# Attention weights written out by head through three buffers, a narrower second form of the value tails, and the lists judged at the last step's end

## The chip, the cores and the metric

The kernel runs on one core of one Trainium2 chip. The metric is the device time of one execution in microseconds (us). Before the change it took 1482.36 us (median of three runs, 1481.56 to 1483.75).

The core's engines work side by side, each in the order of its own queue: TensorE (PE; its weight loads are listed as PEld), VectorE (DVE), ScalarE (ACT), GpSimd (POOL), and SyncE (SP), which issues all of this kernel's DMAs. An engine that waits holds up everything queued behind it on that engine.

## The reference

Attention that keeps the 32 largest scores of every row, and then a two-layer MLP with the SmeLU function. Shapes: batch 8, heads 8, sequence 576, head size 64; the MLP goes from 512 to 2048 and back.

```python
scores = scale * np.matmul(q, k.transpose(0, 1, 3, 2))
kth = np.partition(scores, -top_k, axis=-1)[..., -top_k:-top_k + 1]
mask = scores >= kth
scores = np.where(mask, scores, -1000000000.0)
scores = scores - np.max(scores, axis=-1, keepdims=True)
attn = np.exp(scores)
attn = attn / (np.sum(attn, axis=-1, keepdims=True) + 1e-09)
attn_out = np.matmul(attn, v)
x = attn_out.transpose(0, 2, 1, 3).reshape(B * S, H * D)
h = x @ w_in
g = np.where(h >= 1, h, np.where(h <= -1, 0.0, (h + 1) ** 2 / 4.0))
out = g @ w_out
```

## The kernel before

**Steps.** A sequence of 576 rows is four tiles of 128 rows (t = 0 to 3) and a tail of 64 (t = NT = 4). A step treats one tile of rows for two heads, or in a tail for four heads, two of them in each half of the partitions. There are 144 steps. The batches go in pairs: four tiles of the first batch, the tails of both, then four tiles of the second. `i` counts the two rows of work that lie side by side in a step's tiles `s` (scores) and `e` (weights).

**One step, engine by engine.** PE multiplies queries by keys (L358) and ACT copies the scores to `s` (L359). DVE folds each row in two halves of 288 (`more` and `less`, L372) and looks for the 32 largest with MAX8 and MATCH_REPLACE8 (L379, L392 to L446). ACT takes the exponential (L395). A scan over the two sorted lists (L451) gives the 32nd value, and L458 keeps the weights at or above it and adds them up. POOL divides by the sum (L411) and notes in `excess` whether the lists were long enough (L414).

**How the weights are turned.** The product with the values needs the weights transposed. In the first steps and in the last two (`by_tensor`), PE does this with a diagonal of the reciprocal sums (`diag`, made by ACT at L408, then L473 and L479). In the other 134 steps `move_w` does it through memory: ACT copies the two rows' weights, split in their upper and lower 16 bits, to one tile `halves` (L488, one copy for each `i`); SP writes this tile to DRAM as `rows` (L490) and reads it back transposed as `wT` (L492), once `rows` has landed. Tiles of one tag share buffers: `halves` and `diag` are both of the tag "halves", with one buffer. `wT` has four, `rows` three.

**Products and MLP.** `values` multiplies `wT` by the values (`po`, L506 for the four tiles and L514 for the tails), ACT copies the outcome to `xT` (L519, L521). Once all heads of a tile of rows are there, `mlp` adds its work to a list: `hidden` (`ph`, L539, with its functions on ACT L550 and L558 and on POOL L565 to L568) and `final` (`py`, L578). The output `y` (L581) leaves by SP (L583).

**Tails of the values.** The last 64 rows of the values lie in two forms for each batch. In `v_tl[0]` the even heads lie in partitions 0 to 63 and the odd ones in 64 to 127 (L198, two loads). In `v_tl[1]` the pairs of heads alternate between the two halves (L203, four loads, with a `yield` after each second one). The other half of the partitions is zero in both. The four tiles take the first form, the tails' steps the second. `v_tails` (L84) holds two sets, for even and odd batches.

**Order.** The order on PE, DVE, ACT and POOL is written out by hand: a loop over the steps m, with seven slots in each. `weights` runs a piece of DVE's work in each slot; slot 1 holds `transpose_w`, slot 3 `move_w` of the step before, slot 2 the scores and values. In each slot `advance` takes as much of the MLP's list as the step's share allows, by counted costs, so the MLP is spread over the steps. Keys and queries of the batches from the third on are turned through memory too: `turn` copies them by ACT (`parts`, L283), SP writes them (L285) and reads them back transposed (L292). The loads of keys (L303 to L307), values (L195 to L203) and queries (L211) lie in SP's queue between the steps' transposes, most of them around the change from one pair of batches to the next.

**Judging the lists.** `judge` subtracts counts for the MLP's weights (L864), takes the largest entry of `excess` on DVE (L865), turns it on PE (`pworst`, L867), and takes the largest again (L869). The `flag` that comes of it decides at the very end whether the whole is done once more in a slower way. `judge` is called in slot 2 at m = n, after the last step's diagonals were multiplied and before its values.

Of the kernel before, what the change touches and what calls it, by code (L numbers as in the profile page):

```python
# [11 lines left out]
F32 = mybir.dt.float32  # L12
U16 = mybir.dt.uint16
# [13 lines left out]
def kernel(  # L27
# [10 lines left out]
    nc = tc.nc  # L38
    B, H, S, D = q.shape
    NTOK, DM = out.shape  # L40
    DFF = moe_w_in.shape[1]
    P = 128
# [3 lines left out]
    NHP = H // 2  # L46
    NT = S // P
    SM = NT * P
    TL = S - SM
# [10 lines left out]
    const = ctx.enter_context(tc.tile_pool(name="const", bufs=1))  # L60
# [20 lines left out]

    v_tails = []
    for i in range(2):
        v_tails.append([const.tile([P, H, D], F32, name=f"v_tail{i}{x}") for x in range(2)])  # L84
        for x in v_tails[i]:
            nc.gpsimd.memset(x, 0.0)

# [89 lines left out]
    def run(ctx, paired):  # L177
# [4 lines left out]
        dram = ctx.enter_context(tc.tile_pool(name="dram", bufs=3, space=bass.MemoryType.DRAM))  # L182
# [3 lines left out]
        def whole(x, b):  # L186

            return x[b, :, 0:SM, :].rearrange("h (p c) d -> p h c d", c=NT)

        def load_values(b):  # L190
            v_in = stage.tile([P, H, NT, D], F32, name="v_in")
            v_tl = v_tails[b % 2]
            yield v_in, v_tl
            for h in range(0, H, 2):
                nc.sync.dma_start(out=v_in[:, h:h + 2], in_=whole(v, b)[:, h:h + 2])  # L195
                yield
            for j in range(2):
                nc.sync.dma_start(out=v_tl[0][j * TL:(j + 1) * TL, j::2, :],  # L198
                                  in_=v[b, j::2, SM:S, :].rearrange("h p d -> p h d"))
            yield  # L200
            for hp in range(NHP):
                g = hp % 2
                nc.sync.dma_start(out=v_tl[1][g * TL:(g + 1) * TL, 2 * hp:2 * hp + 2, :],  # L203
                                  in_=v[b, 2 * hp:2 * hp + 2, SM:S, :].rearrange("h p d -> p h d"))
                if g:
                    yield

        def load_queries(b, t):
            if t < NT:
# [14 lines left out]
        def part(i, j):  # L224
            return slice(0, TL) if i == j else slice(TL, P)
# [64 lines left out]
        def finish_turns():  # L290
            while turns:
                turns.pop(0)()  # L292
# [109 lines left out]
        def divide(st):  # L402
            rz = att.tile([P, 2], F32, name="rz")
            nc.vector.reciprocal(rz, st["z"])  # L404
            if st["by_tensor"]:
                st["rz"] = diag = (late or words).tile([P, 2, P], F32, name="diag", tag="halves", bufs=1)
                for i in range(2):
                    nc.scalar.activation(diag[:, i, :], ident, AF.Copy, scale=rz[:, i:i + 1])  # L408
            else:
                for i in range(2):  # L410
                    nc.gpsimd.tensor_scalar(st["e"][:, i, :], st["e"][:, i, :], rz[:, i:i + 1], 1.0, ALU.mult, ALU.mult)  # L411
            if paired:
                m, seconds, kth = st["m"], st["seconds"], st["kth"]
                nc.gpsimd.tensor_tensor(out=excess[:, 2 * m:2 * m + 2], in0=seconds[:, 8:9 + SPLIT:SPLIT], in1=kth[:, LAST:7:-SPLIT],  # L414
                                        op=ALU.subtract)

        def weights(st, before, after):
# [44 lines left out]
            if after is None:  # L462
                divide(st)
# [19 lines left out]

        def move_w(st):
            st["wT"] = wT = late.tile([P, BLOCKS, P], F32, name="wT", bufs=4)
            halves = late.tile([P, 2, 2 * S], U16, name="halves")
            for i in range(2):
                nc.scalar.copy(halves[:, :, i * S:(i + 1) * S], st["e"][:, i, :].bitcast(U16).rearrange("p (k t) -> p t k", t=2))  # L488
            rows = dram.tile([P, 2, 2 * S], U16, name="rows")
            nc.sync.dma_start(out=rows, in_=halves)  # L490
            finish_turns()
            nc.sync.dma_start_transpose(wT.bitcast(U16), rows.rearrange("p t k -> (p t) k"))  # L492

        def block(i, c):
            return i * (NT + 1) + c if c < NT else NT


        def values(st):
            t, hp, v_in, v_tl = st["t"], st["hp"], st["keys"]["v"], st["keys"]["v_tl"]
            wT = st["wT"]  # L500
            po = ps.tile([P, P], F32, name="po", tag="ph", bufs=3)
            if t < NT:
                for c in range(NT + 1):
                    for j in range(2):
                        h = 2 * hp + j
                        nc.tensor.matmul(po[j * D:(j + 1) * D], v_in[:, h, c, :] if c < NT else v_tl[0][:, h, :],  # L506
                                         wT[:, block(j, c)], start=(c == 0), stop=(c == NT))
            else:
                for i in range(2):
                    cols = slice(i * TL, (i + 1) * TL)  # L510
                    for c in range(NT + 1):
                        for j in range(2):
                            h = 2 * (hp + i) + j
                            nc.tensor.matmul(po[j * D:(j + 1) * D, cols], v_in[:, h, c, :] if c < NT else v_tl[1][:, h, :],  # L514
                                             wT[:, block(i, c), part(i, j)],
                                             start=(c == 0), stop=(c == NT))
            xT, col = st["xT"]
            if t < NT:
                nc.scalar.copy(xT[:, hp, col:col + P], po)  # L519
            else:  # L520
                nc.scalar.copy(xT[:, hp:hp + 2, col:col + TL], po.rearrange("p (i n) -> p i n", i=2))  # L521
# [80 lines left out]
        for b in range(0, B, 2):  # L602
            a, c, tl = [(b, t) for t in range(NT)], [(b + 1, t) for t in range(NT)], (b, NT)
# [9 lines left out]
        n = len(steps)  # L613
# [5 lines left out]
        words, late = conversion.enter_context(tc.tile_pool(name="words", bufs=1)), None  # L619
# [32 lines left out]
        K_TIME, PIECE_TIME, UNIT_TIME, SLOTS, EARLY_SHARE = 10.1, 0.9, 0.218, 7, 48  # L652
# [113 lines left out]
        for m in range(n + 2):  # L766
# [3 lines left out]
            elif not early and late is None:  # L770
                conversion.close()
                room.clear()
                late = ctx.enter_context(tc.tile_pool(name="late", bufs=1))
# [15 lines left out]
            for slot in range(SLOTS):  # L789
# [17 lines left out]
                    ready_at[m - 1] = done[m - 1] + 15.0  # L807
                if slot == 3:
                    finish_turns()
                if slot == 2 and m == n and paired:  # L810
                    judge(ps, att)
                if slot == 2 and (early or m == first_late or m >= n - 1):
                    values_until(m)
# [48 lines left out]
    def judge(ps, att):  # L862
        worst = att.tile([P, 8], F32, name="worst", bufs=1)
        nc.vector.tensor_tensor(out=excess[:, 2 * n_steps:], in0=signs[:, 0], in1=signs[:, 1], op=ALU.subtract)  # L864
        nc.vector.max(out=worst, in_=excess)  # L865
        pt = ps.tile([1, P], F32, name="pworst", tag="a", bufs=2)
        nc.tensor.transpose(pt, worst[:, 0:1], ident)  # L867
        top = att.tile([1, 8], F32, name="top8", bufs=1)
        nc.vector.max(out=top, in_=pt)  # L869
        nc.vector.tensor_scalar(flag, top, 0.0, None, ALU.is_gt)  # L870
# [34 lines left out]
```

## Time and profile before

| what | value |
|---|---|
| median of three runs | 1482.36 us |
| the profiled execution | 1484.11 us |
| its span, first to last instruction | 1482.2 us |
| mean granted TensorE clock | 0.992 |
| HBM read, written | 62.91 MB, 102.63 MB |

A group's line has the source line, engine and operation, output<-input, shapes and count, then busy time in all and the mean of one in ns, then the idle time before it:

```profile
L488 ACT COPY halves<-e 128x1152 uint16<-128x1152 uint16 x268 | 293.6, 1143 | 18.5 <-DMA rows<-halves 18.1
L411 POOL TENSOR_SCALAR e<-e,rz 128x576 f32<-128x576 f32 x268 | 235.9, 890 | 13.2 <-DVE rz L404 13.2
```

The list of DMA issues gives the count, the size of one, and the median time from issue to landing in us:

```profile
rows<-halves SPq DMA_DIRECT2D x134, 576.0 KB, 3.3
...
wT<-rows SPq DMA_TRANSPOSE x134, 4.7
...
v_tail<-in_v_dram SPq DMA_DIRECT2D x16, 64.0 KB, 3.9
v_tail<-in_v_dram SPq DMA_DIRECT2D x32, 32.0 KB, 3.4
```

In a timeline a line starts with the start and the duration in us; the bracket at its end holds the idle time before and what ended it. "SPq" is SP's queue: the time is that of issuing, not of the transfer.

### The profile page before, as it was taken

The page shows a single profiled execution, that of the slowest core. Times are in us where ns is not written, and L with a number is a line of the kernel's source. Part 1 is how long each engine was busy: PE and PEld are TensorE (multiplying, and loading weights), DVE is VectorE, ACT ScalarE, POOL GpSimd, SP SyncE. Part 2 cuts the span into 40 slices and gives each one's busy share as a digit, 9 for nine tenths or more (in the row PEclk, how much of TensorE's full clock was granted, in tenths as well). Part 3 has the DMA queues.
Part 4 walks back from the last instruction along what each step waited for, and adds up shares of the span by engine and source line. Part 5 has one row for each costly group of instructions (what it writes and reads, how often), then busy time and mean ns, then how long its engine had stood idle before and what let it go on. Part 6 is the DMA issues. An engine that isn't in the chain of part 4 may idle for free.

```text
span 1482.2 us, 32086 instructions
## 1 busy us (share of the span) xinstructions
PE 1435.8 (97%) x10755; PEld 1044.6 (70%) x10755; DVE 1403.9 (95%) x4392; ACT 1158.0 (78%) x2221; POOL 926.6 (63%) x1310
## 2 busy tenths in 40 slices
PE   6998899999999999999999999999999999999998
PEld 5766677777777777767777777677777777777675
DVE  6989999999999999999999999999999999999912
ACT  7987877878888887887778888788778888777632
POOL 3474566776676666566766677567666666666730
PEclk8999999999999999999999999999999999999999
DMA  8633657775677767787677787787677886665510
GB/s 252 196 121 107 177 152 203 196 194 162 167 206 204 193 193 205 193 209 174 163 195 203 196 198 194 195 214 183 174 197 187 202 202 167 168 166 142 149 25 17
DMA packets 510319, 260.94 MB, mean 176 GB/s; under 512 B 460992, under 2 KB 469184, under 8 KB 510144
## 3 DMA queue, kind: packets, MB, share of 16 engines
q1 hardware_dynamic: 510144, 258.80, 66.4%
q8 instruction: 87, 1.43, 0.4%
q14 instruction: 88, 0.72, 0.2%
HBM read 62.91 MB, written 102.63 MB: 112 GB/s over the span
## 4 chain that ended last, share of the span: by engine, by line
PE 80%; DVE 10%; DMA 4%; ACT 4%; issue 2%; SPq 1%; ACTq 0%; DVEq 0%
PE ph L539 30%; PE py L578 29%; PE sp L358 9%; PE po L506 9%; DVE more L379 2%; DMA rows<-halves 2%; DVE e L458 2%; DMA wT<-rows 1%; PE po L514 1%; DVE more L372 1%; DVE tops L420 1%; DVE tops L428 1%; DVE tops L392 1%; PE pw L473 1%; ACT halves L488 1%
## 5 line engine op out<-in xcount | busy, mean ns | idle before, releaser
L539 PEld LDWEIGHTS ph<-xT,w_in 128*128 128x128 f32 x4608 | 547.0, 192 | 102.6 <-issue 71.1
L539 PE MATMUL ph<-xT,w_in 128*128 128x128 f32 x4608 | 555.7, 276 | 2.3 <-ACT g L558 1.4
L578 PE MATMUL py<-w_out,g 128*128 128x512 f32 x1152 | 541.5, 597 | 1.8 <-ACT y L581 1.8
L565 POOL TENSOR_SCALAR r<-r 128x256 f32<-128x256 f32 x280 | 166.9, 596 | 413.4 <-ACT r L550 409.7
L379 DVE MATCH_REPLACE8 more<-tops,more 128x288 f32<-128x288 f32 x864 | 375.1, 437 | 0.0
L578 PEld LDWEIGHTS py<-w_out,g 128*128 128x128 f32 x1152 | 199.0, 191 | 166.5 <-issue 163.8
L488 ACT COPY halves<-e 128x1152 uint16<-128x1152 uint16 x268 | 293.6, 1143 | 18.5 <-DMA rows<-halves 18.1
L568 POOL TENSOR_TENSOR g<-r,g 128x256 f32<-128x256 f32 x280 | 241.6, 863 | 22.0
L458 DVE SCALAR_TENSOR_TENSOR e<-s,kth,e 128x577 f32<-128x577 f32 x288 | 246.9, 893 | 0.1
L411 POOL TENSOR_SCALAR e<-e,rz 128x576 f32<-128x576 f32 x268 | 235.9, 890 | 13.2 <-DVE rz L404 13.2
L395 ACT ACTIVATE e<-s,nmax 128x576 f32<-128x576 f32 x288 | 222.5, 773 | 4.7
L550 ACT ACTIVATE r<-ph,half 128x256 f32<-128x256 f32 (+1 forms) x296 | 136.1, 460 | 107.8 <-PE ph L539 99.7
L359 ACT ACTIVATE s<-sp 128x576 f32<-128x576 f32 x288 | 171.9, 649 | 61.7 <-PE sp L358 57.7
L567 POOL TENSOR_TENSOR r<-r 128x256 f32<-128x256 f32 x276 | 183.1, 663 | 23.0
L358 PE MATMUL sp<-kT,qT 64*128 64x288 f32 x1024 | 163.1, 436 | 8.3 <-ACT kT L261 6.1
L506 PE MATMUL po<-wT,v_in 128*64 128x128 f32 x2048 | 138.8, 277 | 8.0 <-DMA wT<-rows 4.6
L358 PEld LDWEIGHTS sp<-kT,qT 64*128 64x128 f32 x1024 | 90.0, 189 | 79.3 <-issue 37.2
L506 PEld LDWEIGHTS po<-wT,v_in 128*64 128x64 f32 x2048 | 113.6, 137 | 32.4 <-issue 10.3
L558 ACT ACTIVATE g<-ph,minus 128x256 f32<-128x256 f32 x280 | 130.4, 466 | 0.0
L372 DVE TENSOR_TENSOR more<-s 128x576 f32<-128x576 f32 x144 | 124.1, 862 | 6.0 <-ACT s L359 6.0
L420 DVE MAX8 tops<-more 128x8 f32<-128x288 f32 x288 | 125.4, 443 | 0.0
L372 DVE TENSOR_TENSOR less<-s 128x576 f32<-128x576 f32 x144 | 117.7, 817 | 0.0
(91 smaller groups left out, 1370.0 us busy)
## 6 DMA issues: line engine op xcount, KB each, us to landing
rows<-halves SPq DMA_DIRECT2D x134, 576.0 KB, 3.3
lines<-parts SPq DMA_DIRECT2D x48, 256.0 KB, 3.1
q_in<-in_q_dram SPq DMA_DIRECT2D x32, 256.0 KB, 3.8
v_in<-in_v_dram SPq DMA_DIRECT2D x32, 256.0 KB, 4.5
out_dram<-y SPq DMA_DIRECT2D x32, 256.0 KB, 3.9
raw<-in_moe_w_in_dram SPq DMA_DIRECT2D x32, 256.0 KB, 3.3
raw<-in_moe_w_out_dram SPq DMA_DIRECT2D x32, 256.0 KB, 3.5
kT<-in_moe_w_in_dram SPq DMA_DIRECT2D x8, 512.0 KB, 5.2
```

What stands on the lines that cost most here:

```text
L358: nc.tensor.matmul(*x, start=True, stop=True)
L372: nc.vector.tensor_tensor(out=x, in0=s[:, :, 0:SH], in1=s[:, :, SH:S], op=op)
L379: nc.vector.match_replace(out=st["rest"][:, i, :], in_to_replace=eight(st["tops"], i, r - 8), in_values=src[:, i, :], imm_value=LOWEST)
L395: nc.scalar.activation(e[:, i, :], s[:, i, :], AF.Exp, bias=nmax[:, i:i + 1])
L411: nc.gpsimd.tensor_scalar(st["e"][:, i, :], st["e"][:, i, :], rz[:, i:i + 1], 1.0, ALU.mult, ALU.mult)
L458: nc.vector.scalar_tensor_tensor(out=st["all"][1][:, i, :], in0=st["all"][0][:, i, :], scalar=last[i], in1=st["all"][1][:, i, :], op0=ALU. ...
L488: nc.scalar.copy(halves[:, :, i * S:(i + 1) * S], st["e"][:, i, :].bitcast(U16).rearrange("p (k t) -> p t k", t=2))
L506: nc.tensor.matmul(po[j * D:(j + 1) * D], v_in[:, h, c, :] if c < NT else v_tl[0][:, h, :], wT[:, block(j, c)], start=(c == 0), stop=(c == ...
L539: nc.tensor.matmul(ph[:, i], w_in[:, kk, f * P:(f + 1) * P], xT[:, kk], start=(kk == 0), stop=(kk == NK - 1))
L567: nc.gpsimd.tensor_tensor(out=r, in0=r, in1=r, op=ALU.mult)
L568: nc.gpsimd.tensor_tensor(out=g, in0=r, in1=g, op=ALU.add)
L578: nc.tensor.matmul(py[0], gs[f // group][:, f % group], w_out[:, f, :], start=(f == 0), stop=(f == NF - 1))
```

## The change

The tile `halves` holds one row of work (`i`) instead of two, has three buffers, and each is written to its half of `rows` by a DMA of its own, right after its copy. `diag` shares these three buffers. The second form of the value tails keeps only the four heads (1, 2, 5, 6) that lie in the other half of the partitions than in the first form, and is loaded by two DMAs; a new function `tail_values` chooses the form by head. `judge` is called in the last slot of the last step (m = n + 1), after the last values.

```diff
-        v_tails.append([const.tile([P, H, D], F32, name=f"v_tail{i}{x}") for x in range(2)])
+        v_tails.append([const.tile([P, H // (x + 1), D], F32, name=f"v_tail{i}{x}") for x in range(2)])
...
             yield
-            for hp in range(NHP):
-                g = hp % 2
-                nc.sync.dma_start(out=v_tl[1][g * TL:(g + 1) * TL, 2 * hp:2 * hp + 2, :],
-                                  in_=v[b, 2 * hp:2 * hp + 2, SM:S, :].rearrange("h p d -> p h d"))
-                if g:
-                    yield
+            for x in range(2):
+                nc.sync.dma_start(out=v_tl[1][x * TL:(x + 1) * TL, x::2, :],
+                                  in_=v[b, x + 1::4, SM:S, :].rearrange("h p d -> p h d"))
+            yield
+
+        def tail_values(v_tl, h, t):
+
+            if t == NT and h % 2 != h // 2 % 2:
+                return v_tl[1][:, h // 4 * 2 + h // 2 % 2, :]
+            return v_tl[0][:, h, :]
...
-                st["rz"] = diag = (late or words).tile([P, 2, P], F32, name="diag", tag="halves", bufs=1)
+                st["rz"] = diag = (late or words).tile([P, 2, P], F32, name="diag", tag="halves",
+                                                          bufs=3 if late else 1)
...
         def move_w(st):
             st["wT"] = wT = late.tile([P, BLOCKS, P], F32, name="wT", bufs=4)
-            halves = late.tile([P, 2, 2 * S], U16, name="halves")
+            rows = dram.tile([P, 2, 2 * S], U16, name="rows")
             for i in range(2):
-                nc.scalar.copy(halves[:, :, i * S:(i + 1) * S], st["e"][:, i, :].bitcast(U16).rearrange("p (k t) -> p t k", t=2))
-            rows = dram.tile([P, 2, 2 * S], U16, name="rows")
-            nc.sync.dma_start(out=rows, in_=halves)
+                halves = late.tile([P, 2, S], U16, name="halves", bufs=3)
+                nc.scalar.copy(halves, st["e"][:, i, :].bitcast(U16).rearrange("p (k t) -> p t k", t=2))
+                nc.sync.dma_start(out=rows[:, :, i * S:(i + 1) * S], in_=halves)
             finish_turns()
...
-                        nc.tensor.matmul(po[j * D:(j + 1) * D], v_in[:, h, c, :] if c < NT else v_tl[0][:, h, :],
+                        nc.tensor.matmul(po[j * D:(j + 1) * D], v_in[:, h, c, :] if c < NT else tail_values(v_tl, h, t),
...
-                            nc.tensor.matmul(po[j * D:(j + 1) * D, cols], v_in[:, h, c, :] if c < NT else v_tl[1][:, h, :],
+                            nc.tensor.matmul(po[j * D:(j + 1) * D, cols], v_in[:, h, c, :] if c < NT else tail_values(v_tl, h, t),
...
-                if slot == 2 and m == n and paired:
+                if slot == SLOTS - 1 and m == n + 1 and paired:
                     judge(ps, att)
```

## The prediction, made before the changed kernel was run

> **What bounds the kernel now.** I read the page's totals first, then the chain that ended last, then the waits of each engine, then the timelines of SP, ACT and PE where those waits lie.
>
> ```profile
> PE 1435.8 (97%) x10755; PEld 1044.6 (70%) x10755; DVE 1403.9 (95%) x4392; ACT 1158.0 (78%) x2221; POOL 926.6 (63%) x1310
> ...
> PE 80%; DVE 10%; DMA 4%; ACT 4%; issue 2%; SPq 1%; ACTq 0%; DVEq 0%
> ```
> ```profile
> 1160.00:1180.00 20.00, 20.00 (x137) 13.80 (x136) 20.00 (x63) 15.73 (x30) 11.98 (x18) 1.00 0.89 200
> ```
> ```profile
> 1080.54 0.20 DVE L451 TENSOR_TENSOR_SCAN kth<-tops,seconds 128x25 f32<-128x25 f32 x1
> ...
> 1382.79 0.23 DVE L451 TENSOR_TENSOR_SCAN kth<-tops,seconds 128x25 f32<-128x25 f32 x1
> ```
>
> PE is 97% busy, and the chain runs on PE for 80% of the span. The third line is one of the stretches of 20 us (PE, PEld, DVE, ACT, POOL, clock, DMA share): PE and DVE are both full. The two scans, one per step, lie 32 steps apart: 302.25 / 32 = 9.445 us a step. I set the end of each step's score copy (L359) beside its first use (L372): DVE finds the scores 4 us old or older from 200 us on, so it never waits for PE. Over these 32 steps the scores are ready every 9.444 us, the same period. So PE sets the pace, and DVE, whose quickest steps take 9.14 us, falls in with it. Time is won where PE stands still, if DVE follows.
>
> Where does PE stand still? After 200 us in three kinds of place. First, the passages from one pair of batches to the next (near 240, 590 to 640, 940 us), where SP's queue is behind:
>
> ```profile
> 243.27 2.62 SPq L203 DMA_DIRECT2D v_tail<-in_v_dram  x4
> 246.00 0.52 SPq L490 DMA_DIRECT2D rows<-halves  x1
> ...
> 606.13 2.60 SPq L203 DMA_DIRECT2D v_tail<-in_v_dram  x4
> 608.83 0.54 SPq L490 DMA_DIRECT2D rows<-halves  x1
> ...
> 634.03 2.47 SPq L492 DMA_TRANSPOSE wT<-rows  x1
> ```
> ```profile
> 638.66 1.21 PE L506 MATMUL po<-wT,v_in 128*64 128x128 f32 x16 [2.52 <-ACT parts L283]
> ```
>
> Four loads of the tails' second form take 2.6 us of SP directly ahead of a rows write. The transpose issued at 634.03 lands 4.5 us later, at the moment PE goes on, so the 2.52 us belong to the DMA although ACT is named. The other waits there are 1.07 (254.36), 1.34 (597.07), 0.74 (619.15), 1.95 (945.53) and 0.69 us (967.05). Second, ACT waits for the one halves buffer in these passages, 18.1 us in 12 places:
>
> ```profile
> 634.09 2.21 ACT L488 COPY halves<-e 128x1152 uint16<-128x1152 uint16 x2 [2.74 <-DMA rows<-halves]
> ```
>
> Third, the end:
>
> ```profile
> 1405.01 2.78 DMA rows<-halves
> ...
> 1407.84 4.81 DMA wT<-rows
> ```
> ```profile
> 1408.35 2.05 PE L473 MATMUL pw<-diag,e 128*128 128x128 f32 x16 [2.13 <-ACT diag L408]
> ...
> 1412.79 1.09 PE L506 MATMUL po<-wT,v_in 128*64 128x128 f32 x16 [0.93 <-DMA wT<-rows]
> ...
> 1421.84 0.27 PE L867 MATMUL pworst<-ident,worst 128*1 128x128 f32 x1 [0.79 <-ACT wT L476]
> ```
>
> From 1423 us on PE works through what is left of the MLP without a wait; nothing of the change touches that.
>
> **What the Trainium skill says.** "DMA: Bandwidth & Descriptors", "Anatomy of one DMA": most of a transfer's fixed time is the receipt of the write, not the setup. The trace agrees in kind: a 64 KB key block lands after a median 2.8 us, 576 KB of rows after 3.3. The same page, "Two DMAs through the same engine are not ordered": a DMA that reads what another wrote needs the issuing engine to wait for that one's completion. Here that is SP in front of L492, 301.9 us in 117 waits, with every later DMA behind it. "SBUF — State Buffer", "Who interferes with whom": a DVE instruction with two SBUF inputs blocks against a GpSimd instruction that reads SBUF. The trace shows L372 at 0.74 us alone and 1.20 us at 1397.90, beside a POOL operation; so DVE's steps depend on where POOL's work falls. "TensorE: Matmul & The Clock Gate", "What's actually happening": the clock follows recent activity. Here the granted clock is 0.71 in 640 to 645 us, after the 2.52 us wait, and 0.67 in 945 to 950, after the 1.95; each costs some 1.5 us more.
>
> **The change part by part.** Signs: minus is time saved.
>
> *Rows by head.* The two ACT copies of a step stay (1.15 us each). The single rows DMA becomes two of half the size: 134 more issues of about 0.36 us (the median of L490), 48 us of SP in all. Normally SP arrives early and waits for ACT, so the first half's issue lies under the second copy. The trace's packet records show 128 packets of 4608 B, 178 ns each: 8 per engine, 1.42 us, of the 2.8 us that the quickest takes; 1.4 us is fixed. By head a run in DRAM is 1152 B (576 x 2). From 46 ns for 1024 B I estimate 52 ns, so a half is 16 packets per engine, 0.83 us. The second half lands 1.4 + 0.83 = 2.2 us after its issue: 0.55 us sooner than now. Where SP is late, both are issued one after the other: 0.37 + 1.4 + 0.83 = 2.6 us if the engines are free of the first by then, but the data of both (1.66) and the fixed part give 3.1: 0.26 us later than now. Bounds: from 0.55 won to 0.85 lost per step (two issues of the dearer 0.6 us that L203 shows).
> In the steady stretches the transposed weights land 1.7 us or more before PE takes them, so neither sign shows. It shows where PE waits for them: at 159.71 (3.34) and 176.16 us (0.37), where the write follows ACT at once: -0.6 together. At the end, -0.55. At 597.07 and 945.53, where SP is late and the tail loads lie behind the rows write: +0.3 each, +0.6.
>
> *Three buffers.* Two buffers hold a step, the third takes the next step's first copy, so most of the 18.1 us of ACT goes. ACT is not the bound; what it held back on PE are the 0.74 us (scores) and 0.69 us (r): I take half of both, -0.7, between 0 and -1.4. The diagonals at the end no longer wait for a halves buffer. ACT would make them at 1406.4 instead of 1407.9, but PE then only stands longer at the next line, for the transposed weights: 0. Cover gone would make it worth at most 1.5.
>
> *Tails.* Two loads of half as many heads in all instead of four: 1.3 us less of SP per batch. It counts directly ahead of a rows write. At 243.27: 1.3 less 0.26 is 1.0, capped by PE's 1.07: I take -0.9. At 606.13: -1.3, given back three times 0.26 until 634.03: -0.5, and -0.5 of clock loss with a shorter idle. At 953.79 likewise, but the waits behind are 0.69 or less: -0.3. Smaller memsets: POOL's first real work starts at 10.66, long after them: 0. The choice of tile in the product changes no matmul.
>
> *Lists judged later.* On DVE, subtract and MAX8 (0.7 us) move to after the last values; DVE has nothing else there. On PE, pworst no longer stands between pwt and po, where it waited 0.79 us for a PSUM buffer. But po needs the same ACT copy, ended at 1421.78, and so gains 0.2; the transpose itself (0.27) comes later. I take -0.2, between 0 and -0.8. The flag is read after 1476 us, so the later verdict costs nothing.
>
> Sum: -0.6 - 0.55 + 0.6 - 0.7 - 0.9 - 1.0 - 0.3 - 0.2 = -3.65. The profiled execution was 1484.11 us with a span of 1482.2: 1.9 us lie around it. It gives 1480.5, and against the median of 1482.36, 1478.7.
>
> **Rivals.**
> *A, as summed: 1478.7.* For it: each of these waits is PE's, and PE sets the pace. Against: DVE must follow. It is full to 1411.6, and with DVE unmoved only about 2 us can be won at the end (POOL ends the weights of the third last step at 1401.02, ACT copies them from 1402.79).
> *B, hidden: 1481.4.* The extra issues give back in the passages what the tails save, DVE doesn't follow, and 0.75 to 1 us at the end stays. For it: SP is issuing or waiting all through 577 to 634 us.
> *C, slower: 1486.4.* The second half makes SP later in the passages: with 0.85 us a step over three steps, 2.55 us less 1.3 from the tails. PE then waits 1.3 us more in each of three passages, and each idle costs about as much again in clock, 0.3 us of it here: 3 x 1.6 = 4.8; less the 0.75 at the end, about +4. It decides from some 0.45 us a late step. For it: the costs of SP from the trace. Against: the first half is on its way earlier.
> *D, DVE is set free: 1473.* Near 618 to 775 us DVE takes 9.75 us a step, 0.3 over the locked period, in 16 steps: 4.9 us; 0.2 in eight steps near 930: 1.5. If smoother passages avoid these collisions, 6 us go beside the end's 2 to 3. The same mechanism can also cost: 9.55 instead of 9.445 for 40 steps adds 4; that widens the range upwards.
>
> **How the numbers follow.** A 0.38, D 0.12, B 0.30, C 0.20. A difference below about 0.2% (3 us) can't be told from none here. A and D are faster by more (0.50), B is same (0.30), C slower (0.20). The range from 1472 to 1486 reaches over D and the nearer part of C.
>
> **What would show it.** Right: the halves waits gone from ACT, SP's tail loads in twos, PE's waits at 254 and 638 shorter, rows landing 2.2 us after the second issue at the end. Wrong: PE's waits for the transposed weights grown in the passages, or DVE's steps longer than 9.5 us with POOL's operations beside L372 and L458; or PE's waits gone and the end where it was, which would mean that DVE, not PE, leads.

## The result, and the profile after

The changed kernel takes 1500.78 us (median of five runs, 1497.67 to 1503.88), beside 1483.66 us for the kernel before on the same chip: a ratio of 1.0113, 95% interval 1.0094 to 1.0132. The forecast was 1478.7. The profiled execution is the longest of the five (1503.88 us); its span is 1502.0 us, 19.8 more than before, so what follows adds up to some 20 us, not to 17.

The page's totals, and the shares of the chain that ended last:

```profile
PE 1440.8 (96%) x10755; PEld 1047.8 (70%) x10755; DVE 1418.4 (94%) x4392; ACT 1157.8 (77%) x2221; POOL 919.8 (61%) x1310
...
PE 80%; DVE 9%; DMA 6%; ACT 3%; issue 1%; SPq 0%; ACTq 0%; DVEq 0%
```

No engine has more instructions than before. PE still carries the chain; its idle time is now 61.2 us instead of 46.4, and its busy time 5.0 us more. The waits (us in total, times, and the longest in us):

```profile
PE po L511 <- DMA wT<-rows: 24.5, 10, 4.7
```
```profile
SPq L497 <- DMA rows<-halves: 281.0, 133, 4.0
```

The first was 4.6 us before, in three times, and 2.5 more that the view puts down to ACT (at 638.66): PE now waits ten times for transposed weights. The second, SP standing in front of the transpose until the rows have landed, was 301.9.

Where was the time lost? The scans of DVE, one per step, at steps 41, 73, 105 and 137 (start and duration in us, from the timeline):

```profile
440.92 0.20 DVE L456 TENSOR_TENSOR_SCAN kth<-tops,seconds 128x25 f32<-128x25 f32 x1
...
754.18 0.20 DVE L456 TENSOR_TENSOR_SCAN kth<-tops,seconds 128x25 f32<-128x25 f32 x1
...
1072.64 0.47 DVE L456 TENSOR_TENSOR_SCAN kth<-tops,seconds 128x25 f32<-128x25 f32 x1
...
1375.16 0.29 DVE L456 TENSOR_TENSOR_SCAN kth<-tops,seconds 128x25 f32<-128x25 f32 x1
```

The same four before:

```profile
438.67 0.20 DVE L451 TENSOR_TENSOR_SCAN kth<-tops,seconds 128x25 f32<-128x25 f32 x1
...
745.23 0.41 DVE L451 TENSOR_TENSOR_SCAN kth<-tops,seconds 128x25 f32<-128x25 f32 x1
...
1052.23 0.40 DVE L451 TENSOR_TENSOR_SCAN kth<-tops,seconds 128x25 f32<-128x25 f32 x1
...
1354.67 0.30 DVE L451 TENSOR_TENSOR_SCAN kth<-tops,seconds 128x25 f32<-128x25 f32 x1
```

So 2.3 us are lost up to step 41, 6.7 in the next 32 steps, 11.5 in the 32 after them, and nothing from step 105 on: 302.5 us for 32 steps in both kernels. The loss is spread over 64 steps and isn't confined to the passages between pairs of batches. It shows as PE's waits there:

```profile
486.45 1.09 PE L511 MATMUL po<-wT,v_in 128*64 128x128 f32 x16 [2.36 <-DMA wT<-rows]
...
527.66 1.98 PE L511 MATMUL po<-wT,v_in 128*64 128x128 f32 x16 [3.25 <-DMA wT<-rows]
...
648.90 1.23 PE L511 MATMUL po<-wT,v_in 128*64 128x128 f32 x16 [3.88 <-DMA wT<-rows]
...
883.29 1.98 PE L511 MATMUL po<-wT,v_in 128*64 128x128 f32 x16 [4.69 <-DMA wT<-rows]
```

The wait at 648.90 is the one that was 2.52 at 638.66; those at 486, 527 and 883 are new. In the step of the wait at 486.45 the rows are written 16.9 us after DVE's last weights, against 11.6 before, and the transposed weights land at 24.8 instead of 19.4.

Part of the loss is clock. In the 10 us behind the waits at 527.66, 648.90 and 883.29 the mean granted TensorE clock was 0.70, 0.83 and 0.73, which by itself is an estimated 7.4 us of lost clock; before, behind the waits at 638.66 and 945.53, it was 0.83 twice, 3.4 us. The difference of 4 us is most of the 5.0 us that PE is busy for longer with the same matmuls.

DVE's busy time grew by 14.5 us: the mean of L463 went from 893 to 916 ns (7 us in all) and that of `less` in L376 from 817 to 886 (10 us), of which `more` gives back 4. That DVE and POOL meet in other places once PE is late is the likely reason; it is not shown by itself, but DVE's busy time is 1396.0 us in hand_v_halves below, where the same two writes stand and PE's waits for the transposed weights of L511 are down to 6.1 us.

The rows writes in the list of DMA issues, and one line's own view (issue time of one, min/median/max in ns):

```profile
rows<-halves SPq DMA_DIRECT2D x268, 288.0 KB, 3.1
```
```profile
L495 SPq DMA_DIRECT2D rows<-halves x268: 533/564/1486, 139.2 to 1425.5; - x134
```

Before, it was 332/362/606 for 134 writes. Summed over the records, SP spent 156.0 us on issuing rows instead of 52.6, and 823.7 instead of 726.7 on all its DMAs.

At the end, the first idle line was 2.13 and the second 0.93 before; `pworst` had 0.79:

```profile
1427.20 2.05 PE L478 MATMUL pw<-diag,e 128*128 128x128 f32 x16 [0.51 <-ACT diag L413]
...
1432.82 1.09 PE L511 MATMUL po<-wT,v_in 128*64 128x128 f32 x16 [2.10 <-DMA wT<-rows]
...
1443.10 0.27 PE L872 MATMUL pworst<-ident,worst 128*1 128x128 f32 x1
```

### The profile page after: what moved, and what is told of

Its sections match the earlier page's. It is cut to its first block, busy times and chain, and to the rows that moved or that the text cites. A ratio compares the mean times of both kernels' runs of the same rounds, so it can differ in the third digit from the quotient of the medians.

```text
span 1502.0 us, 32396 instructions
## 1 busy us (share of the span) xinstructions
PE 1440.8 (96%) x10755; PEld 1047.8 (70%) x10755; DVE 1418.4 (94%) x4392; ACT 1157.8 (77%) x2221; POOL 919.8 (61%) x1310
## 4 chain that ended last, share of the span: by engine, by line
PE 80%; DVE 9%; DMA 6%; ACT 3%; issue 1%; SPq 0%; ACTq 0%; DVEq 0%
PE ph L544 31%; PE py L583 30%; PE sp L362 9%; PE po L511 9%; DMA wT<-rows 3%; DVE more L383 2%; DVE e L463 2%; PE po L519 1%; DMA rows<-halves 1%; DVE more L376 1%; PE pw L478 1%; DVE tops L425 1%; DVE tops L433 1%; DVE tops L396 1%; DVE tops L444 1%
## 5 line engine op out<-in xcount | busy, mean ns | idle before, releaser
L570 POOL TENSOR_SCALAR r<-r 128x256 f32<-128x256 f32 x280 | 155.0, 553 | 439.6 <-ACT r L555 435.9
L494 ACT COPY halves<-e 128x1152 uint16<-128x1152 uint16 x268 | 294.5, 1142 | 11.2 <-DMA rows<-halves 10.9
L573 POOL TENSOR_TENSOR g<-r,g 128x256 f32<-128x256 f32 x280 | 245.8, 878 | 22.0
L463 DVE SCALAR_TENSOR_TENSOR e<-s,kth,e 128x577 f32<-128x577 f32 x288 | 253.9, 916 | 4.9 <-ACT e L399 4.8
L416 POOL TENSOR_SCALAR e<-e,rz 128x576 f32<-128x576 f32 x268 | 226.2, 854 | 13.2 <-DVE rz L408 13.2
L572 POOL TENSOR_TENSOR r<-r 128x256 f32<-128x256 f32 x276 | 195.6, 709 | 23.0
L511 PE MATMUL po<-wT,v_in 128*64 128x128 f32 x2048 | 141.2, 279 | 26.3 <-DMA wT<-rows 24.5
L511 PEld LDWEIGHTS po<-wT,v_in 128*64 128x64 f32 x2048 | 115.0, 138 | 52.2 <-issue 18.6
L563 ACT ACTIVATE g<-ph,minus 128x256 f32<-128x256 f32 x280 | 130.2, 465 | 0.0
L376 DVE TENSOR_TENSOR less<-s 128x576 f32<-128x576 f32 x144 | 127.6, 886 | 0.0
L376 DVE TENSOR_TENSOR more<-s 128x576 f32<-128x576 f32 x144 | 120.0, 834 | 7.3 <-ACT s L363 7.3
```

The lines of the kernel that those rows point to most:

```text
L376: nc.vector.tensor_tensor(out=x, in0=s[:, :, 0:SH], in1=s[:, :, SH:S], op=op)
L463: nc.vector.scalar_tensor_tensor(out=st["all"][1][:, i, :], in0=st["all"][0][:, i, :], scalar=last[i], in1=st["all"][1][:, i, :], op0=ALU. ...
L494: nc.scalar.copy(halves, st["e"][:, i, :].bitcast(U16).rearrange("p (k t) -> p t k", t=2))
L572: nc.gpsimd.tensor_tensor(out=r, in0=r, in1=r, op=ALU.mult)
L573: nc.gpsimd.tensor_tensor(out=g, in0=r, in1=g, op=ALU.add)
```

## The experiments

Three theories at first: Q, the second write's issue on SP; P, the shorter packets of 1152 bytes; T, the tails, the later judging or the third buffer. Ratios are to the kernel before, run beside each; its medians there lie between 1478.84 and 1483.69 us. So kernels that were not run beside each other are compared by their ratios.

### Parts of the change

*tails_alone* has only the tails' part of the diff; *tails_judge* adds the later judging, with `move_w` as before. *split_two* is the kernel before with the write split and two buffers for `halves` and `diag`:

```diff
-            nc.sync.dma_start(out=rows, in_=halves)
+            for i in range(2):
+                halves = late.tile([P, 2, S], U16, name="halves", bufs=2)
+                nc.scalar.copy(halves, ...)
+                nc.sync.dma_start(out=rows[:, :, i * S:(i + 1) * S], in_=halves)
```

> The kernel before with the tails' second form in two loads and nothing else. Q: 1.3 us of SP less in each passage at the place where PE waits: 1 to 3 us faster than before, like tails_judge; the judging is worth 0.2 us at most, which this comparison can't show.

> The kernel before with the tails' second form in two loads and the late judging, but with its one rows write per step. Theory Q (SP's queue: a step's rows are issued in 0.36 us before, in two times 0.56 us after, so the transposes come late): none of the loss is in these parts; 2 to 4 us faster than before, about 1480. Theory P (the packets of 1152 B keep the DMA engines longer): the same. Theory T (the loss comes from the tails or the judging): slower by 5 us or more.

> The kernel before with the rows by head alone, in two buffers of one head (the memory of before), tails and judging as before. Q and P: the whole loss or more is here, since the tails give nothing back to SP: 17 to 30 us slower than before. T: no loss, within 5 us of before. If the third buffer were what costs, within 5 us of before too.

Measured: 1480.92 us, 0.9993 (0.9986 to 1.0); 1480.54 us, 0.9990 (0.9980 to 1.0); 1510.01 us, 1.0188 (1.0160 to 1.0216). T falls: those parts win 1 to 1.5 us. The loss comes with the split of the write: 28 us with two buffers here; 17 us are lost in the changed kernel, which has three buffers and the small gain of the tails.

### Who issues, and in which pieces

*act_issue_halves* is the changed kernel with both halves issued by ACT; *act_issue_whole* is tails_judge with the one write issued by ACT. *one_dma_short_runs* is tails_judge with one DMA in packets of 1152 bytes, *split_partitions* with two DMAs in packets of 4608:

```diff
-                nc.sync.dma_start(out=rows[:, :, i * S:(i + 1) * S], in_=halves)
+                nc.scalar.dma_start(out=rows[:, :, i * S:(i + 1) * S], in_=halves)
```
```diff
+            halves = late.tile([P, 2, 2, S + 8], U16, name="halves")
...
+            nc.sync.dma_start(out=rows.rearrange("p t (i k) -> p (t i) k", i=2),
+                              in_=halves.rearrange("p t i k -> p (t i) k")[:, :, 0:S])
```
```diff
+            for p in range(0, P, P // 2):
+                nc.sync.dma_start(out=rows[p:p + P // 2], in_=halves[p:p + P // 2])
```

> The changed kernel with both halves' writes issued by ACT, right behind their copies, instead of by SP: the same packets, 156 us less of issuing on SP, some 1.2 us more on ACT in a step. Q: the loss goes; 1482 or less, if ACT bears the issues. P: it stays near 1500, since the packets are the same. If ACT's issues block it for long, it is slower than 1500.

> One whole rows write per step, issued by ACT behind the second copy; tails in two loads, late judging. Q: SP is freed of the rows altogether, so PE's waits for the weights in the passages (about 8 us before) shrink: 1470 to 1478. P: the same as with SP's issue, about 1480.

> Tails and late judging, one rows write per step, but from a tile with a gap of 16 bytes behind every 576 halves, so that it goes in 512 packets of 1152 bytes as in the changed kernel. Q: the issue is single (0.4 to 0.6 us), so at most 0.2 us more of SP per step: within 5 us of tails_judge. P: the data of a step takes the DMA engines as long as in the changed kernel: 12 us or more slower than tails_judge.

> Tails and late judging, the rows write cut in two by partitions (64 and 64), each in whole packets of 4608 bytes, both behind the second copy: twice the issues, packets as before. Q: SP issues for about 0.7 us a step instead of 0.36, less than half of what the change adds: 2 to 10 us slower than tails_judge. P: equal to tails_judge.

Measured: act_issue_halves 1506.74 us, 1.0162 (1.0138 to 1.0186). SP's issues fell to 663.8 us, but ACT now spent 0.54 us on each of 268, and PE waited 11.0 us for ACT's L563 in front of the values; so it doesn't tell Q and P apart. act_issue_whole 1486.1 us, 1.0026 (1.0012 to 1.0040), 0.34 us for each issue on ACT: a miss for Q, which had 1470 to 1478, though here too ACT pays.

one_dma_short_runs 1490.6 us, 1.0050 (1.0033 to 1.0067): the issue took 0.59 us instead of 0.36, 25 us of SP in all, and the kernel is some 9 us over tails_judge, more than Q had and less than P had. split_partitions 1504.51 us, 1.0145 (1.0126 to 1.0163). Two writes lose as much with long packets as with short ones, but these long packets moved slower (308 us per DMA engine in all, 196 before), so P isn't ruled out here. hand_v_halves below is the stronger evidence: it has the short packets and hardly loses.

### A spare transfer

*extra_issue* puts a spare DMA from a constant tile ahead of the whole rows write of tails_judge; *extra_issue_bound* reads it from `halves`:

```diff
+            spare = dram.tile([P, 2, 4], U16, name="spare")
+            nc.sync.dma_start(out=spare[:, :, 0:2], in_=halves[:, :, 0:2])
             nc.sync.dma_start(out=rows, in_=halves)
```

> Tails and late judging, one whole rows write, and ahead of it in SP's queue one more DMA with two runs per partition of 4 bytes, from a constant: nearly no data and nothing waits for it, but SP issues for some 0.56 us more in each of 134 steps (the change adds 0.76). Q: most of the loss comes back without any short packet of the weights: 8 to 20 us slower than the kernel before. P: within 3 us of tails_judge (1480.5).

> extra_issue mended: tails_judge with the same spare transfer out of the halves buffer ahead of the rows write, SP's order left to the scheduler, which keeps half the loads between rows write and transpose. Q: slower than tails_judge by 10 to 20 us, with PE waiting for wT in the steps from 40 to 100. If the loss lies in the data or the second completion: within 3 us of tails_judge (1480.5).

Measured: 1536.73 us, 1.0352, and 1720.91 us, 1.1616 (1.1596 to 1.1635). Both are misses as experiments. In extra_issue nothing tied the spare DMA to its step, and all 134 were issued in groups between 25 and 242 us, most of them long before their steps; PE waited 28.5 us there for keys. In the bound form the spare packets of 4 bytes are cheap themselves (9 ns), but the run says nothing of an issue alone: the rows landed late, as the records of its sister below show.

But extra_issue raised another question. SP's queue is not among the four whose order the code fixes; the scheduler orders it. Was that order the same in all these kernels? Counting, between each rows write and its transpose, what SP issues there (it has to wait there for the landing anyway), gives another queue wherever there are two writes: of the loads of key blocks and queries, 41 stood in that wait before and in tails_judge, 4 in the changed kernel and in split_two. Theory O: the order is the loss.

Two kernels above speak against O as the whole cause. split_partitions has 81 such loads in the wait and is slow all the same. And one_dma_short_runs issues its transfers in exactly the order of tails_judge, yet loses some 9 us: in that order, a dearer issue with shorter packets costs without any reordering.

### One order, with one write and with two

Adding SP to the engines of fixed order makes SP issue in the order of the code, the same in each kernel but for the second write. *sp_hand_whole* does so with tails_judge, *sp_hand_halves* with the changed kernel; *sp_hand_extra* and *sp_hand_extra512* add the spare transfer to the first, with runs of 4 and of 512 bytes. *cover_whole* and *cover_halves* put the loads of the late stage in the wait.

```diff
-                                            mybir.EngineType.Pool})
+                                            mybir.EngineType.Pool, mybir.EngineType.SP})
```
```diff
         def finish_turns():
+            while loads_due:
+                loads_due.pop(0)()
             while turns:
                 turns.pop(0)()
+
+        def load_later(**x):
+            loads_due.append(partial(nc.sync.dma_start, **x))
...
-                    nc.sync.dma_start(out=x[:, 0::2, :], in_=whole(k, b)[:, 0::2, c, :])
+                    load_later(out=x[:, 0::2, :], in_=whole(k, b)[:, 0::2, c, :])
```

> The kernel of tails_judge (one whole rows write, tails and late judging of the change), with SP added to the engines whose instructions stay in the order in which the code emits them. In the kernels so far SP's order is the scheduler's, and it is not the same in them: with one rows write, 41 loads of key blocks and queries stand between a rows write and its transpose, where SP waits anyway; with two, 4 do. Here no load stands there but raw and v_in parts stand ahead of the rows write. It is the base for the next two. If SP's order matters much (theory O), this kernel is slower than before by 10 us or more, since the loads have left the wait; if only the number of issues matters (Q), it is within 5 us of 1482.

> The changed kernel (two rows writes by head, three buffers) with SP in the order of the code: instruction by instruction the order of sp_hand_whole, with the rows write doubled and nothing else moved. Q, the issue time of the second write makes SP late: 15 to 25 us over sp_hand_whole. O, the order that the scheduler gave SP was the loss: within 5 us of sp_hand_whole.

> sp_hand_whole with one spare transfer per step directly ahead of the rows write: it reads the first four bytes of each head from the halves buffer (so it can't leave its step, as the spare transfer of extra_issue did) and writes them to a spare place in DRAM that nobody reads: 256 packets of 4 bytes, next to no data. The rows write itself is whole, its packets long, nobody waits for the spare one. Q: an issue of about 0.55 us a step alone does it, 10 to 25 us over sp_hand_whole and not far from sp_hand_halves. If the loss lies in the data of the two halves or in waiting for two completions, no more than 3 us over sp_hand_whole.

> sp_hand_extra with runs of 512 bytes in place of 4: one spare transfer of 128 KB a step ahead of the whole rows write, of which nobody waits. By the packets of 256 bytes (18 ns) and 1024 bytes (46 ns) a run of 512 takes some 27 ns, 256 of them 0.43 us on each of 16 engines. If the rows' packets stay near 180 ns and it is 5 to 12 us over sp_hand_whole, the issue alone costs what the second half cost. Under 3 us: the loss lies in the halves' data. If the rows' packets slow down again, the run can't tell.

> sp_hand_whole (SP in the order of the code, one whole rows write), with the loads of key blocks, queries and raw weights of the late stage put between the rows write and the transposes, so that SP issues them while it would wait for the rows to land. If the order's loss is that loads left this wait (O), the 9 us of sp_hand_whole come back: at most 1482, perhaps 1476, since more loads lie there than in the kernel before (41). If it has another cause, it stays within 3 us of sp_hand_whole (1489.5).

> The changed kernel with the same order on SP as cover_whole: two rows writes by head, three buffers, and the loads in the wait for the rows. If SP's time is what the change lacks, it now has it: within 4 us of cover_whole, and faster than the changed kernel by 15 us or more. If two writes cost by their data or by the second completion whatever SP has to do, the 7 us between sp_hand_whole and sp_hand_halves stay.

Measured: sp_hand_whole 1489.53 us, 1.0060 (1.0043 to 1.0076); sp_hand_halves 1496.83, 1.0104 (1.0082 to 1.0125); cover_whole 1491.36, 1.0065 (1.0051 to 1.0078); cover_halves 1497.32, 1.0103 (1.0084 to 1.0122). The second write costs some 6 to 7 us in either order, where Q had 15 to 25; and the loads moved into the wait did not help, so O in this form, the count of loads in the wait, falls too. sp_hand_extra took 1762.76 us, 1.1888: the rows' packets of 4608 bytes took a mean of 440 ns there, not the 190 of sp_hand_whole, so it tells nothing of an issue alone. sp_hand_extra512 took 1511.92, 1.0197 (1.0181 to 1.0212), some 20 us over sp_hand_whole with rows packets of 200 ns: more than expected, with 59 us more of data per DMA engine beside the issue, so it doesn't part the two.

The timeline of SP in sp_hand_whole shows why that order is poor in itself:

```profile
574.39 0.42 SPq L215 DMA_DIRECT2D q_in<-in_q_dram  x1
582.90 0.39 SPq L195 DMA_DIRECT2D v_in<-in_v_dram  x1
583.41 0.40 SPq L587 DMA_DIRECT2D out_dram<-y  x1
583.91 0.37 SPq L494 DMA_DIRECT2D rows<-halves  x1
```

From 574.81 to 582.90 a load of values waits at the head of the queue for its buffer, and the rows write behind it with it. This happens three times (9.2, 8.1 and 7.3 us), and three times in sp_hand_halves and in the two cover kernels as well.

### The order mended, and then broken in one place

*hand_v_whole* and *hand_v_halves* are sp_hand_whole and sp_hand_halves with those loads begun 7 steps later. *turns_first* is hand_v_halves with one line moved:

```diff
+                            if "loads" in got and value_loads is not got["loads"]:
+                                values_from = m + 7 if m < n and steps[m][1] == NT else m
...
-                    elif value_loads is not None:
+                    elif value_loads is not None and m >= values_from:
```
```diff
             rows = dram.tile([P, 2, 2 * S], U16, name="rows")
+            finish_turns()
             for i in range(2):
...
-            finish_turns()
             nc.sync.dma_start_transpose(wT.bitcast(U16), rows.rearrange("p t k -> (p t) k"))
```

> sp_hand_whole with the loads of the values begun 7 steps later in those passages where they waited for their buffer (the first batch of a new pair). If the three waits of 7 to 9 us with the rows write behind them were the 9 us, this is back at 1480 to 1483; if it stays at 1487 or more, the order has another fault.

> The changed kernel (two rows writes by head, three buffers) in the order of hand_v_whole, instruction for instruction but for the second write. Theory Q in its present form: the second write costs SP some 0.8 us a step in any order, and that costs the kernel 5 to 8 us over hand_v_whole; the rest of the changed kernel's loss was the order in which the scheduler put SP's transfers round two writes. So some 1487 to 1490, faster than the changed kernel by 10 us or more. If the second write alone makes the whole loss, it is 15 us or more over hand_v_whole; if the order alone does, within 3 us.

> hand_v_halves with one line moved: the transposes of turned keys and queries (60, of 1.3 us or more, each behind a wait for its lines to land) are issued ahead of the step's rows writes, as the scheduler has them in the changed kernel for 53 of 60, in place of behind them, where SP waits for the rows anyway. If this is what the scheduler's order lacked, most of the 20 us come back: 1490 to 1500, with the rows writes of steps 41 to 60 and 73 to 100 late by 3 to 5 us. If it is another difference of the orders (the key blocks and queries behind the transposed weights stand there in both), it stays within 4 us of hand_v_halves (1477.9).

Measured: hand_v_whole 1476.40 us, 0.9976 (0.9965 to 0.9987); hand_v_halves 1477.92 us, 0.9986 (0.9977 to 0.9996); turns_first 1530.21 us, 1.0310 (1.0285 to 1.0334). With the order mended, the whole changed kernel is no slower than before, and the second write costs 1.5 us (the intervals overlap). One line then costs some 48 us by the ratios.

SP's timeline before, at the step in which the changed kernel has its first long wait; then in the changed kernel, and in hand_v_halves:

```profile
463.77 0.33 SPq L285 DMA_DIRECT2D lines<-parts  x1
464.15 0.45 SPq L303 DMA_DIRECT2D k_block<-in_k_dram  x1
466.51 2.49 SPq L492 DMA_TRANSPOSE wT<-rows  x1
469.04 0.62 SPq L304 DMA_DIRECT2D k_block<-in_k_dram  x1
469.70 0.62 SPq L307 DMA_DIRECT2D k_block<-in_k_dram  x1
470.42 1.27 SPq L292 DMA_TRANSPOSE kT<-lines  x1
471.79 0.53 SPq L490 DMA_DIRECT2D rows<-halves  x1
475.11 2.41 SPq L492 DMA_TRANSPOSE wT<-rows  x1
```

```profile
471.86 2.43 SPq L497 DMA_TRANSPOSE wT<-rows  x1
474.35 0.58 SPq L307 DMA_DIRECT2D k_block<-in_k_dram  x1
474.98 0.68 SPq L308 DMA_DIRECT2D k_block<-in_k_dram  x1
475.70 0.65 SPq L311 DMA_DIRECT2D k_block<-in_k_dram  x1
476.45 1.28 SPq L296 DMA_TRANSPOSE kT<-lines  x1
477.77 1.26 SPq L495 DMA_DIRECT2D rows<-halves  x2
481.81 2.30 SPq L497 DMA_TRANSPOSE wT<-rows  x1
```
```profile
465.91 2.15 SPq L497 DMA_TRANSPOSE wT<-rows  x1
468.11 0.58 SPq L289 DMA_DIRECT2D lines<-parts  x1
468.74 0.42 SPq L307 DMA_DIRECT2D k_block<-in_k_dram  x1
469.20 0.68 SPq L308 DMA_DIRECT2D k_block<-in_k_dram  x1
469.93 0.65 SPq L311 DMA_DIRECT2D k_block<-in_k_dram  x1
470.63 0.60 SPq L134 DMA_DIRECT2D raw<-in_moe_w_in_dram  x1
471.28 1.28 SPq L495 DMA_DIRECT2D rows<-halves  x2
472.66 1.43 SPq L296 DMA_TRANSPOSE kT<-lines  x1
475.80 2.49 SPq L497 DMA_TRANSPOSE wT<-rows  x1
```

Before and in the changed kernel the rows leave behind the transpose of the turned keys (`kT<-lines`), and SP then stands idle until they have landed. What differs is how late the queue runs: before, one of the key blocks lies in the wait of the step ahead, and the rows leave 1.3 us after ACT's second copy; in the changed kernel all three key blocks come behind that wait, and the second write leaves 6.2 us after the copy. In hand_v_halves the turned keys' transpose lies in the wait. The waits of SP for the landing of the rows, hand_v_halves first, then turns_first:

```profile
SPq L497 <- DMA rows<-halves: 264.5, 147, 3.5
```
```profile
SPq L497 <- DMA rows<-halves: 377.7, 142, 5.1
```

Summed over the issue records between a step's first rows write and its transpose. "Loads" are those of key blocks and queries; "rows late" is the time from the end of ACT's second copy to the start of the step's last rows write, summed over the 134 steps:

| kernel | rows writes a step | loads in the wait | turned transposes in the wait, of 60 | issues in the wait, us in all | rows late, us in all | ratio |
|---|---|---|---|---|---|---|
| hand_v_whole | 1 | 0 | 60 | 106.5 | 24 | 0.9976 |
| tails_judge | 1 | 41 | 3 | 58.3 | 114 | 0.9990 |
| before | 1 | 41 | 3 | 58.3 | 108 | 1 |
| one_dma_short_runs | 1 | 41 | 3 | 69.7 | 134 | 1.0050 |
| hand_v_halves | 2 | 0 | 60 | 95.1 | 79 | 0.9986 |
| cover_halves | 2 | 119 | 60 | 212.4 | 71 | 1.0103 |
| sp_hand_halves | 2 | 0 | 60 | 93.3 | 186 | 1.0104 |
| changed | 2 | 4 | 7 | 54.4 | 218 | 1.0113 |
| split_partitions | 2 | 81 | 8 | 171.4 | 215 | 1.0145 |
| split_two | 2 | 4 | 7 | 52.1 | 207 | 1.0188 |
| turns_first | 2 | 0 | 0 | 0 | 350 | 1.0310 |

What lies in the wait doesn't order the kernels with two writes. How late the rows leave orders them better: 79 us in the one that hardly loses, some 190 to 220 in those that lose 1 to 2%, 350 in the slowest. cover_halves is the exception; it still has the three stops at the head of the queue. This is a relation seen over these runs; only turns_first and hand_v_halves differ in one thing alone, and no kernel with one write was run with the line moved.

## Why the prediction was wrong, step by step

- **The step that failed** is the zero for the steady stretches: "In the steady stretches the transposed weights land 1.7 us or more before PE takes them, so neither sign shows", with the one before it, "Normally SP arrives early and waits for ACT". The sum counted late rows in two passages (+0.6). In steps 41 to 60 and 73 to 100 the rows write came 4.8 us later in its step on average (3.0 of it with ACT's copies, which by then ended later too), and the slack at every second step, up to 6.2 us before, was eaten. Steps 41 to 104 lost 18.2 of the 20 us.
- **The reading under it was not sound either.** In the kernel before, the transposed weights of steps 47 and 83 land only 1.06 and 0.26 us before PE takes them, and the waits of 3.25 and 4.69 us are at just these two steps. Nor was SP always early: before, the rows write left more than 1 us after ACT's second copy in 39 of 134 steps; in the changed kernel in 56.
- **Behind it lay a term never asked about: SP's order.** The prediction took the order of before, and moved nothing in it. The scheduler made another: 4 loads instead of 41 in the wait. The turned transposes are not the difference: 57 of 60 stood outside the wait before, and 53 in the changed kernel. In an order fixed by hand and mended, the same two writes cost 1.5 us, as "neither sign shows" would have it. What two writes cost in exactly the order of before was not tried; the nearest is one_dma_short_runs, in which one dearer write cost some 9 us.
- **A term mis-sized:** the half's issue was taken at 0.36 us and 48 us more in all; it was 0.56, and 103 more. The bound of 0.85 us lost a step was worked out with 0.6 us for an issue; but lateness in a queue adds up from step to step (the rows came 0.9, 2.4 and 5.4 us later in steps 41, 42 and 43), and no bound for one step holds it.
- **Right in kind:** a 1152 byte packet takes 51 ns (52 predicted). At 159.71 us the wait went from 3.34 to 2.85, and in the last turned step the transposed weights land 17.4 us after DVE's weights instead of 17.9: half a microsecond each, as forecast. That is luck in part: at the end the rows land 2.5 us after the second issue, not 2.2 (2.8 before), and the rest came from a quicker transpose. At 176.16 nothing was won (0.46 instead of 0.37). At the end the diagonal's wait shrank and the next one grew, as said.
- **Three buffers:** ACT's waits for `halves` fell from 18.1 to 10.9 us only; in split_two, with two, they are 20.8. The tails and the judging win 1 to 1.5 us where 2.4 were predicted, at the edge of what the runs resolve. Where the tail loads counted most, PE's wait grew from 1.07 to 2.18 (at 255.51): the rows' first issue came at 246.0 us as before, since the queue ahead of it had grown, and the transpose was issued at 250.80 instead of 249.25.
- **Rivals:** C had the mechanism, SP later by the second half, but in the passages alone, at +4 instead of +17. The reverse of D, DVE's steps growing longer, came on top. "PE's waits for the transposed weights grown in the passages" was named as a sign of being wrong; they grew there, and more outside.

The Trainium skill's page "DMA: Bandwidth & Descriptors", section "Two DMAs through the same engine are not ordered", which the prediction drew on, explains why SP must stand between rows and transpose. The traces put that wait at 301.9 us before, and at 264.5 us in hand_v_halves and 377.7 in turns_first; the last two issue the same transfers and differ in the place of the turned transposes alone.

Shown is that two writes cost 1.5 us in one order of SP's queue, 6 to 7 in another, and 17 to 28 in the orders that the scheduler made. Open stays how much of the changed kernel's loss belongs to the new order, how much to the 103 us of issues, and how much to the shorter packets. turns_first shows how much one difference of order can make; it is not the difference between before and the changed kernel.

## What to carry to other kernels

Where a queue must wait for a transfer to land, issue there what needs nothing of it: 60 transposes moved out of that wait by one line cost some 48 us. Before pricing an added DMA, find out whether the order of its queue is fixed or will be made anew, and compare the two orders before the times. Look at the smallest slack in a stretch, not at the usual one. The fixed order with one write (hand_v_whole, 0.9976) is the best version of this study, 0.24% under the kernel before.

## What the hardware showed that was not expected

- The issue of a DMA on SP has a price by shape: in the kernel before, the whole rows write took 0.33 to 0.37 us alone and 0.35 to 0.61 right behind another issue; in the changed kernel a half (two runs per partition in DRAM) never under 0.53; in split_partitions a write of 64 partitions took a median of 0.58. Issued by ACT, the whole write and a half hold ACT for 0.34 and 0.54.
- Packets of 4 bytes, 9 ns each, ahead of the rows write made its packets take 440 ns on average (sp_hand_extra; the median stayed at 181, so some took far longer), and the rows land after a median of 6.6 us. Spare transfers of the same size that lay elsewhere (extra_issue) left the packets at 185.
- Cut by partitions (split_partitions), packets of the same 4608 bytes took 308 us per DMA engine in all instead of 196.
- The granted clock doesn't follow the length of a wait of PE alone: behind 1.95 us (945.53, before) it was 0.83 over the next 10 us, and behind 3.27 us (1006.34, changed kernel) it stayed at 1.00.
